# Earlier transfers in the first slots, and a later copy out of PSUM, in a fused attention and MLP kernel

## The chip, the core and the metric

The kernel runs on one core of a Trainium2 chip. The metric is the device time of one execution in microseconds (us); lower is better. PE (TensorE) multiplies matrices into PSUM; DVE (VectorE) and ACT (ScalarE) work element by element and are the ones here that read PSUM; POOL (GpSimd) works on SBUF alone. SP (SyncE), ACT and POOL can each issue DMA transfers, and the transfers that an engine issues stand in that engine's queue.

## The reference

Attention with a sliding window of 128 keys and a linear position bias, over 8 batches of 8 heads, 576 tokens and 64 channels, and on its output an MLP with a hard-swish:

```python
scores = scale * np.matmul(q, k.transpose(0, 1, 3, 2))
mask = (rel >= 0) & (rel < window)
scores = np.where(mask, scores + bias[None], -1000000000.0)
attn = np.exp(scores - max) / sum
x = np.matmul(attn, v)            # heads side by side: 4608 tokens x 512
h = x @ w_in                      # 512 x 2048
g = h * np.clip(h + 3.0, 0.0, 6.0) / 6.0
out = g @ w_out                   # 2048 x 512
```

All inputs and the output are float32 in DRAM; the kernel computes in bf16.

## The kernel before

**Slots.** Two heads are a pair; 32 pairs (8 batches of 4) are numbered g = 0 to 31. The kernel is a written-out order of instructions, one slot for each pair. Slots 0 to 4 are in `first_batch`, slots 5 to 31 in `segment`. In a slot, `scores(g)` computes the score tiles `scd` (diagonal blocks) and `sco` (the others), `exp_diag` and `exp_off` take their exponentials on ACT into `pd`, `po` and `p4buf` and mask them on POOL (L288, L298, L309), and `values(g - 1)` multiplies the pair before with v; DVE divides the result (L335, L336) into `avs`. `back` turns `avs` into columns of `xT`. Each engine does its instructions in the order in which they are written.

**q and k.** The pairs of batches 0 to 2 (g = 0 to 11) are loaded as contiguous runs with a cast to bf16 by `load_pairs` on POOL's DMA queue; `prepare(g)` reorders them in SBUF (`pr`, L217), `transposes(g)` turns them on PE (L234), and copies on DVE or ACT (L238) bring them from PSUM into `qTb` and `kTb`. For g of 9 to 11 both transposed tiles lie in one PSUM tile `tpp` of the pool `ps_sc`, which has two buffers and also serves `scd` and `sco`. From batch 3 on, q and k come as tokens over SP's queue (`load_tokens`, L121, five pieces of up to 256 KB), POOL casts them into the single buffer `tbuf` (L195), and a DMA transpose on SP (`xbar`, L200) writes `qTb` or `kTb`. So a cast into `tbuf` waits until the DMA transpose before it has read it. All v go over SP's queue too.

**Buffers.** `ldbuf[0]` to `ldbuf[3]` take all these loads in turn. `ldbuf[3]` holds pair 0 of batch 0 (`wide`) and then v of batch 1. In `stage_next(0)` a POOL memset of one element of `ldbuf[3]` stands ahead of the loads of v of batch 1, so that SP issues these only after POOL has come to it.

**MLP.** `moe_up` is four matmuls into `hps` (pool `ps_h`, two buffers), a ReLU on ACT into `r` (L373) and a DVE instruction into `g` (L374); `moe_down` is four matmuls (L401). These 288 units are taken in a fixed order by `fill`, in numbers fixed for each place of a slot: two in slot 4, then 4, 4, 3 and 3 in slots 5 to 8, eight in each later slot, and the rest at the end. A unit of 512 tokens needs the attention of those tokens done.

**Loads ahead.** `stage_next(g)` at the end of slot g issues loads: in slot 0 pairs 4 and 5 and v of batch 1, in slot 1 the first quarter of w_in, in slot 2 pairs 6 and 7, in slot 3 the second quarter of w_in, and so on until w_out has been loaded in slots 6 to 8. Weights and the pairs of the first three batches share POOL's queue, tokens and DMA transposes share SP's.

Of the kernel before, what the change touches and what calls it, by code (L numbers as in the profile page):

```python
# [18 lines left out]
def kernel(  # L19
# [9 lines left out]
    nc = tc.nc  # L29
    B, H, S, D = q.shape  # L30
# [5 lines left out]
    NP = H // 2  # L36
    NQ = 5
    LAST = S - 4 * 128
    SP = NQ * 128
    W = D + 1  # L40
# [70 lines left out]
    def flush(b=None, nm=None):  # L111
        while todo and (b is None or any(x[0] == (b, nm) for x in todo)):
            todo.pop(0)[1]()
# [12 lines left out]
    def constants():  # L126
        nc.vector.memset(bias3, 0.5)
        nc.vector.memset(warm, 0.0)
        nc.scalar.activation(out=warm, in_=warm, func=ACT.Exp)
        make_identity(nc, ident)  # L130
        for nm in "qk":
            load_pairs(0, nm, 1, 2)
        nc.gpsimd.iota(rel_i, pattern=[[0, 1]], base=0, channel_multiplier=1)
        base = rpool.tile([128, NT], FP32, tag="r6", name="base")
        base_i, base_b = base[:, 0:128].bitcast(INT32), base[:, 256:320].bitcast(BF16)
        nc.gpsimd.iota(base_i, pattern=[[0, 128]], base=-64, channel_multiplier=1)
        nc.gpsimd.tensor_copy(out=base_b, in_=base_i)
        nc.gpsimd.affine_select(out=base_b, in_=base_b, pattern=[[1, 128]],
                                channel_multiplier=-1, base=0,
                                compare_op=ALU.is_ge, fill=-(2.0 ** 30))  # L140
        for hp in range(2, NP):
            for nm in "qk":
                load_pairs(0, nm, hp, hp + 1)
        nc.vector.memset(kTb[0][:, :, 4, LAST:128], 0.0)
        nc.vector.memset(vbuf[0][:, :, :, D:W], 1.0)
        nc.vector.memset(vbuf[0][64:128, 4, :, 0:D], 0.0)
        nc.vector.memset(p4buf[0], 1.0)
        for h in range(H):
            nc.vector.tensor_scalar(out=tab[:, h, :], in0=base_b, scalar1=slopes[h] / scale,
                                    scalar2=0.0, op0=ALU.mult, op1=ALU.add)  # L150
        nc.gpsimd.memset(p4buf[1], 1.0)
        nc.gpsimd.memset(kTb[1][:, :, 4, LAST:128], 0.0)
        nc.gpsimd.memset(vbuf[1][:, :, :, D:W], 1.0)
        nc.gpsimd.memset(vbuf[1][64:128, 4, :, 0:D], 0.0)

    def biases():
        nc.vector.tensor_copy(out=rel_f, in_=rel_i)
        for h in range(H):
# [44 lines left out]
    st = {}  # L203
# [17 lines left out]
    def transposes(g):  # L221
        b, hp = divmod(g, NP)
        if g > 2 * NP:
            pair = ps_sc.tile([128, 2, 512], FP32, tag="sc", name="tpp")
        tps = {}
        for nm in "qk":
            src = st.pop((g, nm)).rearrange("p t e d -> p t (e d)")
            if g > 2 * NP:
                tp = pair[:, "qk".index(nm), 0:S // 2].bitcast(BF16).rearrange(
                    "p (t a) -> p t a", t=RT)  # L230
            else:
                tp = ps_h.tile([128, RT, RP], BF16, tag="h", name="tp", padded_shape=[128, 8, 128])
            for t in range(RT):
                nc.tensor.transpose(tp[:, t, :], src[:, t, :], ident[:RP, :RP])  # L234
            tps[nm] = tp
        for nm, dst in (("q", qTb[b % 2]), ("k", kTb[b % 2])):
            eng = nc.scalar.copy if nm == "k" and (g == 0 or g > 2 * NP) else nc.vector.tensor_copy
            eng(out=dst[:, hp, :, :].rearrange("p j c -> p (j c)")[:, 0:S].rearrange(  # L238
                "p (a t) -> p a t", t=RT), in_=tps[nm].rearrange("p t a -> p a t"))

# [194 lines left out]
    def stage_next(g):  # L435
        b, hp = divmod(g, NP)
        if g == 0:
            load_pairs(1, "q", 0, 2)
            load_pairs(1, "k", 0, 2)
            nc.gpsimd.memset(ldbuf[3][0:1, 0:1], 0.0)  # L440
            load_tokens(1, "v")
            flush()
        if g == 1:
            load_w_in(0)
        if g == 2:
            load_pairs(1, "q", 2, NP)
            load_pairs(1, "k", 2, NP)
        if g == 3:
            load_w_in(1)
        if g in (4, 5):  # L450
            load_w_in(g - 2)
            load_pairs(2, "q", 2 * (g - 4), 2 * (g - 3))
            load_pairs(2, "k", 2 * (g - 4), 2 * (g - 3))
        if g == 5:
            load_tokens(2, "v")
        if g == 6:
            load_w_out(0)
            load_w_out(1)
            load_tokens(3, "q")
        if g in (7, 8):  # L460
            load_w_out(g - 5)
        if g == 7:
            cast_tokens(2, "v")
            load_tokens(3, "k")
        if g == 8:
            cast_tokens(3, "q")
        if g == 9:
            load_tokens(3, "v")
            xbar(3, "q")
            cast_tokens(3, "k")  # L470
        if g == 10:
            xbar(3, "k")
            load_tokens(4, "q")
        if g == 11:
            cast_tokens(3, "v")
            load_tokens(4, "k")
            load_tokens(4, "v")
            cast_tokens(4, "q")
        if b >= 3 and b + 1 < B:
            if hp < 2:  # L480
                xbar(b + 1, "qk"[hp])
            if hp in (0, 2):
                cast_tokens(b + 1, "kkv"[hp])
        if b >= 3 and b + 2 < B:
            if hp > 0:
                load_tokens(b + 2, "qkv"[hp - 1])
            if hp == 3:
                cast_tokens(b + 2, "q")
# [6 lines left out]

    def first_batch():
        transposes(0)
        prepare(1)
        biases()
        for g in range(NP):  # L500
            if g != 2:
                scores(g)
            exp_diag(g, 0)
            spin(0)
            transposes(g + 1)
            exp_off(g, 0)
            exp_off(g, 1)
            if g == 1:
                for j in range(NQ):
                    cast_v(0, j, nc.scalar if j < 3 else nc.gpsimd)  # L510
                scores(2)
            prepare(g + 2)
            if g == 1:
                spin(0)
            if g > 0:
                values(g - 1, (0, 1, 2))
                values(g - 1, (3, 4))
            if g > 1:
                back(g - 2)
            if g == 2:  # L520
                more_constants()
            stage_next(g)
        g = NP
        scores(g)
        back(g - 2)
        values(g - 1, (0, 1, 2))
        values(g - 1, (3, 4))
        exp_diag(g, 0)
        for j in range(4):
            cast_v(1, j, nc.gpsimd)  # L530
        exp_off(g, 0)
        exp_off(g, 1)
        transposes(g + 1)
        back(g - 1)
        done[0] = g
        cast_v(1, 4, nc.gpsimd)
        prepare(g + 2)
        fill(1)
        stage_next(g)
        fill(1)  # L540

# [3 lines left out]
    def segment(lo, hi, fills):  # L545
        for g in range(lo, hi + 1):
            f = fills(g)
            if by_xbar(g - 2):
                done[0] = g - 1
            pe_next = g + 1 < hi and (g + 1) // NP < NB_PE  # L550
            if g < hi:
                scores(g)
            if pe_next and g < 2 * NP:
                transposes(g + 1)
            fill(f[0])
            if g < hi:
                exp_diag(g, 0)
            fill(f[1])
            if g < hi:
                exp_diag(g, 1)  # L560
            if g >= lo:
                values(g - 1, (0, 1, 2))
            fill(f[2])
            if pe_next and g >= 2 * NP:
                transposes(g + 1)
            if g < hi:
                exp_off(g, 0)
            fill(f[3])
            if g < hi:
                exp_off(g, 1)  # L570
            if g >= lo:
                values(g - 1, (3, 4))
            fill(f[4])
            if g >= lo:
                back(g - 1)
                if not by_xbar(g - 1):
                    done[0] = g
            if g + 2 < hi and (g + 2) // NP < NB_PE:
                prepare(g + 2)
            fill(f[5])  # L580
            if g < hi:
                stage_next(g)
            fill(f[6])
# [3 lines left out]
    with tc.manual_schedule(engines=every):  # L587
# [6 lines left out]
        for _ in range(30):  # L594
            nc.tensor.matmul(wm, lhsT=ident, rhs=ident, start=True, stop=True)
        prepare(0)
        first_batch()
        segment(NP + 1, G, lambda g: FILLS.get(g, (1, 1, 1, 1, 1, 1, 2)))
        done[0] = G
# [34 lines left out]
```

## Time and profile before

| | us |
|---|---|
| median of 4 runs | 341.62 (340.44 to 342.06) |
| the profiled execution | 341.8 |
| its span, first to last instruction | 340.1 |
| PE busy | 319.3 (94%) |
| ACT busy | 201.0 (59%) |
| DVE busy | 172.4 (51%) |
| POOL busy | 152.5 (45%) |
| granted TensorE clock | 1.000 |

The page cuts the span into 40 equal slices of 8.5 us and gives the busy share of each engine in tenths. The view of waits adds up how long an engine sat idle before an instruction and what released it. The chain of waits is followed back from the last instruction, at each step to what released it. The timeline lists instructions with their start and length, and in brackets the idle time ahead of them. The slots can be told by `scores`: slot 5 begins at 31.0 us, slot 8 at 51.0, 9 at 58.9, 10 at 70.1, 11 at 81.3, 12 at 90.4, 13 at 99.5 and 14 at 107.6. Queue q0 is POOL's, q1 is SP's, q10 is ACT's.

### The profile page before, as it was taken

To read this page: it belongs to the slowest core of one execution; us is meant where nothing else is said; L and a number is where in the kernel's file an instruction comes from. 1 tells how busy PE (TensorE), PEld (TensorE's weight loads), DVE (VectorE), ACT (ScalarE), POOL (GpSimd) and SP (SyncE) were. 2 spreads that over 40 slices of the span, in tenths; PEclk is the share of its full clock that TensorE was granted. 3 is DMA by queue.
4 is the path that set the end of the run, shared out by engine and by line. 5 is a ranking of instruction groups with operands and counts; after the bars stand their busy time and mean duration, and the time that the engine had idled before them with its cause. 6 is when DMAs were issued, how large, how long until landed. Compare 5 with 4: busy or idle time off the path is not lost.

```text
span 340.1 us, 6829 instructions
## 1 busy us (share of the span) xinstructions
PE 319.3 (94%) x2615; PEld 166.7 (49%) x2615; DVE 172.4 (51%) x358; ACT 201.0 (59%) x353; POOL 152.5 (45%) x263
## 2 busy tenths in 40 slices
PE   7887997897999999999999999999999999999995
PEld 5575554453444454554454444554555444444443
DVE  3677885554445455555455454545455444444410
ACT  3778776655657575767576757675765444343401
POOL 8779877635835663667366717632331000000000
PEclk9999999999999999999999999999999999999999
DMA  8999999999999999599959995410111000100021
GB/s 173 186 224 197 196 195 196 217 217 211 227 217 171 210 205 224 135 217 233 230 97 189 239 178 138 98 50 33 54 50 50 33 31 31 64 31 31 33 93 63
DMA packets 134832, 48.15 MB, mean 142 GB/s; under 512 B 121360, under 2 KB 130320, under 8 KB 134800
## 3 DMA queue, kind: packets, MB, share of 16 engines
q1 hardware_dynamic: 122464, 33.89, 55.2%
q0 software_dynamic: 8672, 7.44, 13.8%
q10 hardware_dynamic: 3664, 6.39, 5.5%
q8 instruction: 20, 0.33, 0.4%
q14 instruction: 12, 0.10, 0.1%
HBM read 36.70 MB, written 9.44 MB: 136 GB/s over the span
## 4 chain that ended last, share of the span: by engine, by line
PE 64%; SPq 8%; ACT 7%; DVE 6%; POOL 5%; issue 5%; DMA 3%; POOLq 0%
PE hps L369 28%; PE ops L401 26%; SPq L121 6%; DVE g L374 3%; ACT r L373 3%; ACT po L295 2%; DMA ldbuf<-in_k_dram 2%; POOL pd L288 2%; SPq L200 2%; POOL tbuf L195 2%; PE av L330 2%; PE scd L265 1%; PE av L327 1%; DVE qTb L238 1%; DVE avs L336 1%
## 5 line engine op out<-in xcount | busy, mean ns | idle before, releaser
L374 DVE SCALAR_TENSOR_TENSOR g<-r,hps 128x512 bf16<-128x512 f32 x144 | 99.0, 688 | 137.0 <-ACT r L373 136.9
L373 ACT ACTIVATE r<-hps,bias 128x512 f32<-128x512 f32 x144 | 99.5, 692 | 104.9 <-PE hps L369 102.8
L369 PE MATMUL hps<-xT,w_in_sb 128*128 128x512 bf16 x576 | 146.9, 379 | 9.5 <-DVE g L374 9.3
L401 PE MATMUL ops<-w_out_sb,g 128*128 128x512 bf16 x560 | 141.8, 379 | 0.0
L401 PEld LDWEIGHTS <-g 128*128 128x128 bf16 x560 | 54.3, 98 | 63.5
L369 PEld LDWEIGHTS <-w_in_sb 128*128 128x128 bf16 x576 | 50.8, 97 | 62.5 <-issue 12.6
L298 POOL TENSOR_SCALAR_AFFINE_SELECT po<-po 128x512 bf16<-128x512 bf16 x64 | 40.0, 635 | 22.5 <-ACT po L295 20.0
L288 POOL TENSOR_SCALAR_AFFINE_SELECT pd<-pd 128x512 bf16<-128x512 bf16 x46 | 28.1, 635 | 39.8 <-ACT pd L285 39.8
L195 POOL CAST tbuf<-ldbuf 128x512 bf16<-128x512 f32 (+1 forms) x50 | 28.6, 614 | 36.8 <-issue 25.0
L295 ACT ACTIVATE po<-sco,bias_o 128x512 bf16<-128x512 f32 x64 | 43.1, 689 | 0.0
L336 DVE TENSOR_TENSOR avs<-av,rc 128x384 bf16<-128x384 f32 (+1 forms) x56 | 28.0, 501 | 1.9
L285 ACT ACTIVATE pd<-scd,bias_d 128x512 bf16<-128x512 f32 x46 | 29.0, 685 | 0.0
L330 PEld LDWEIGHTS <-pd 128*128 128x128 bf16 x256 | 19.3, 99 | 9.4 <-issue 0.7
L327 PE MATMUL av<-vbuf,po 128*128 128x65 bf16 x224 | 21.6, 195 | 0.7 <-POOL po L298 0.6
L330 PE MATMUL av<-vbuf,pd 128*128 128x65 bf16 x240 | 22.0, 196 | 0.0
L327 PEld LDWEIGHTS <-po 128*128 128x128 bf16 x256 | 19.5, 100 | 3.9 <-POOL po L298 1.1
L407 ACT COPY osb<-ops 128x512 f32<-128x512 f32 x18 | 10.6, 586 | 12.7 <-PE ops L401 12.6
L217 POOL COPY pr<-ldbuf 96x768 bf16<-96x768 bf16 x17 | 13.7, 822 | 4.6 <-DMA ldbuf<-in_k_dram 3.9
L306 ACT ACTIVATE p4buf<-sco,bias_d 128x64 bf16<-128x64 f32 x46 | 14.9, 324 | 0.0
L409 DVE COPY osb<-ops 128x512 f32<-128x512 f32 x17 | 11.6, 684 | 5.8 <-PE ops L401 5.8
L265 PE MATMUL scd<-qTb,kTb 64*128 64x128 bf16 x256 | 13.3, 227 | 0.0
L234 PE MATMUL tp<-ident,pr 96*128 96x96 bf16 x108 | 9.2, 243 | 3.8 <-POOL pr L217 1.0
(76 smaller groups left out, 222.0 us busy)
## 6 DMA issues: line engine op xcount, KB each, us to landing
ldbuf<-in_v_dram SPq DMA_DIRECT2D x32, 256.0 KB, 5.4
out_dram<-osb ACTq DMA_DIRECT2D x23, 256.0 KB, 3.6
ldbuf<-in_q_dram SPq DMA_DIRECT2D x20, 256.0 KB, 5.2
ldbuf<-in_k_dram SPq DMA_DIRECT2D x20, 256.0 KB, 5.8
out_dram<-osb SPq DMA_DIRECT2D x12, 256.0 KB, 2.0
w_in_sb<-in_moe_w_in_dram POOLq DMA_DIRECT2D x4, 512.0 KB, 8.5
w_out_sb<-in_moe_w_out_dram POOLq DMA_DIRECT2D x4, 512.0 KB, 11.1
ldbuf<-in_q_dram POOLq DMA_DIRECT2D x4, 288.0 KB, 8.8
```

The costliest lines, as they stand in the source:

```text
L195: nc.gpsimd.tensor_copy(out=tbuf[:m, :, j, :], in_=s[:m, j, :, :].rearrange("p (i e) d -> p i (e d)", e=2))
L285: nc.scalar.activation(out=pd[:, e, :, :].rearrange("p j c -> p (j c)"), in_=sc[:, e, :], func=ACT.Exp, bias=bias_d[:, h:h + 1], scale=scale)
L288: nc.gpsimd.affine_select(out=pd[:, e, :, :], in_=pd[:, e, :, :], pattern=[[0, 4], [1, 128]], channel_multiplier=-1, base=0, compare_op=AL ...
L295: nc.scalar.activation(out=po[:, e, :, :].rearrange("p j c -> p (j c)"), in_=sc[:, e, :], func=ACT.Exp, bias=bias_o[:, h:h + 1], scale=scale)
L298: nc.gpsimd.affine_select(out=po[:, e, :, :], in_=po[:, e, :, :], pattern=[[0, 4], [-1, 128]], channel_multiplier=1, base=-1, compare_op=A ...
L327: nc.tensor.matmul(av[:, i, e, :], lhsT=po[:, e, qt - 1, :], rhs=vb[:, qt - 1, h, :], start=True, stop=False)
L330: nc.tensor.matmul(av[:, i, e, :], lhsT=d, rhs=vb[:, qt, h, :], start=(qt == 0), stop=True)
L336: nc.vector.tensor_tensor(out=st[g, "avs"][:, qts[0]:qts[0] + nq, :, :], in0=av[:, 0:nq, :, 0:D], in1=rc[:, 0:nq, :, :].to_broadcast([128, ...
L369: nc.tensor.matmul(hps, lhsT=w_in_sb[:, ks, ts(ms, 128)], rhs=xT[:, ks, ts(nt, NT)], start=(ks == 0), stop=(ks == n_ks - 1))
L373: nc.scalar.activation(out=r6, in_=hps, func=ACT.Relu, bias=bias3[:, 0:1], scale=1.0 / 6.0)
L374: nc.vector.scalar_tensor_tensor(out=gts[nt][:, ms, :], in0=r6, scalar=1.0, in1=hps, op0=ALU.min, op1=ALU.mult)
L401: nc.tensor.matmul(ops[nt, sub], lhsT=gts[nt][:, ms, ts(sub, 128)], rhs=w_out_sb[:, ms, :], start=(ms == 0), stop=(ms == n_ms - 1))
```

## The change

There are four edits. The loads of v of batch 1 move from the end of slot 0 to the place right after `prepare(0)`, and the one-element memset goes. The first quarter of w_in is issued in slot 0 instead of slot 1, and pairs 6 and 7 in slot 1 instead of slot 2. Four memsets of the second set of buffers move from POOL to DVE, ahead of the eight instructions that write `tab`. The copies from PSUM become a function `settle`: for pairs 9, 10 and 11 it runs after the second half of `values` instead of right behind the transposes, and the copy of k, until now on ACT for these pairs, is on DVE like that of q. For all other pairs `settle` follows `transposes` directly, on the same engines as before.

```diff
         nc.vector.memset(p4buf[0], 1.0)
+        nc.vector.memset(p4buf[1], 1.0)
+        nc.vector.memset(kTb[1][:, :, 4, LAST:128], 0.0)
+        nc.vector.memset(vbuf[1][:, :, :, D:W], 1.0)
+        nc.vector.memset(vbuf[1][64:128, 4, :, 0:D], 0.0)
         for h in range(H):
             nc.vector.tensor_scalar(out=tab[:, h, :], in0=base_b, scalar1=slopes[h] / scale,
                                     scalar2=0.0, op0=ALU.mult, op1=ALU.add)
-        nc.gpsimd.memset(p4buf[1], 1.0)
-        nc.gpsimd.memset(kTb[1][:, :, 4, LAST:128], 0.0)
-        nc.gpsimd.memset(vbuf[1][:, :, :, D:W], 1.0)
-        nc.gpsimd.memset(vbuf[1][64:128, 4, :, 0:D], 0.0)
...
             tps[nm] = tp
+        st[g, "tps"] = tps
+
+    def settle(g):
+        b, hp = divmod(g, NP)
+        tps = st.pop((g, "tps"))
         for nm, dst in (("q", qTb[b % 2]), ("k", kTb[b % 2])):
-            eng = nc.scalar.copy if nm == "k" and (g == 0 or g > 2 * NP) else nc.vector.tensor_copy
+            eng = nc.scalar.copy if nm == "k" and g == 0 else nc.vector.tensor_copy
...
         if g == 0:
             load_pairs(1, "q", 0, 2)
             load_pairs(1, "k", 0, 2)
-            nc.gpsimd.memset(ldbuf[3][0:1, 0:1], 0.0)
-            load_tokens(1, "v")
-            flush()
+            load_w_in(0)
         if g == 1:
-            load_w_in(0)
-        if g == 2:
             load_pairs(1, "q", 2, NP)
             load_pairs(1, "k", 2, NP)
...
                 values(g - 1, (3, 4))
+            if pe_next and g >= 2 * NP:
+                settle(g + 1)
             fill(f[4])
...
         prepare(0)
+        load_tokens(1, "v")
+        flush()
         first_batch()
```

## The prediction

> **What bounds the kernel now.** I read the page's slices first.
>
> ```profile
> PE   7887997897999999999999999999999999999995
> DMA  8999999999999999599959995410111000100021
> ```
>
> From the twelfth slice (93 us) on PE is full, so what it does there (2.6 thousand matmuls, none of them touched) keeps its length; the change can only move the start of that stretch. But the DMA engines are full too for the first 24 slices. Next the waits in slots 8 to 11 (50 to 82 us), PE's first, ACT's second:
>
> ```profile
> PE hps L369 <- DVE g L374: 5.8, 4, 1.9
> ```
> ```profile
> ACT kTb L238 <- DVE qTb L238: 4.4, 3, 1.6
> ```
>
> PE stands 5.8 us, in three waits of 1.9 us and a small one. The timeline of slot 9 shows why:
>
> ```profile
> 63.92 0.75 DVE L238 COPY qTb<-tpp 128x576 bf16<-128x576 bf16 x1
> ...
> 64.70 0.64 ACT L238 COPY kTb<-tpp 128x576 bf16<-128x576 bf16 x1 [1.42 <-DVE qTb L238]
> ...
> 65.24 0.69 ACT L295 ACTIVATE po<-sco,bias_o 128x512 bf16<-128x512 f32 x1
> ...
> 66.78 0.72 ACT L373 ACTIVATE r<-hps,bias 128x512 f32<-128x512 f32 x1
> ...
> 67.53 0.69 DVE L374 SCALAR_TENSOR_TENSOR g<-r,hps 128x512 bf16<-128x512 f32 x1 [2.31 <-ACT r L373]
> ...
> 68.27 1.02 PE L369 MATMUL hps<-xT,w_in_sb 128*128 128x512 bf16 x4 [1.85 <-DVE g L374]
> ```
>
> ACT stands 1.42 us at its copy of k until DVE has copied q; both exponentials, r, g and at last PE come late by that and by the copy. Then the chain of waits of 68 to 112 us, to see what a sooner PE meets:
>
> ```profile
> 96.90 1.11 SPq L121
> ...
> 98.20 4.15 SPq L200
> 102.39 3.64 DMA ldbuf<-in_v_dram
> ...
> 108.36 1.18 POOL pd L288 x2
> 109.54 1.19 POOL po L298 x2
> 110.77 0.20 PE av L327
> ```
> ```profile
> 105.52 2.84 POOL L195 CAST tbuf<-ldbuf 128x512 bf16<-128x512 f32 x5 [8.46 <-DMA qTb<-tbuf]
> ```
>
> SP issues loads without a pause up to the DMA transpose of q of batch 4 at 98.20; POOL idles 8.46 us for that one to land, casts k, and only then masks pd and po of slot 13. PE, in slot 14, waits 0.35 us for them at 110.77. So at 110 us two paths arrive almost together: PE's, and SP's queue through `tbuf`. That second one decides my forecast.
>
> **The copies (settle).** Behind the change ACT goes from r straight to the exponentials; both copies follow the second values on DVE. Slot 9 worked out: r ends 63.28; two exponentials and two of p4 (65.24 to 66.9, 1.67) end 64.95; r of the next unit follows its matmuls (65.1) and ends 65.9. DVE: g to 64.0, the division of values (0.17 + 0.42, matmuls done 64.3) to 65.0, q 0.75, k 0.70 (it was 0.64 on ACT, 0.66 as a second copy on DVE in slot 6), then g 0.69 at 66.45 to 67.15. PE goes on at 67.2 instead of 68.27: **1.1 us**. Slot 10 has the same rows 11.16 us on: 1.1. Slot 8 the same way (copies 54.85 to 56.3, g to 57.0 instead of 57.93): 0.9. DVE has the 2 x 0.7 us free (it idles 2.31 ahead of g); if it hadn't, g would be late by them. `tpp` is held 1.5 us longer; the next to want its buffer is sco of the next slot (70.09 less the gain, against 66.4), so nobody waits. Sum 3.1 us.
>
> **The loads.** POOL's queue keeps its order: pairs 4 and 5, w_in's first quarter, pairs 6 and 7, w_in's second. Only the issue moves. w_in's 0.76 us of issue comes at 14.19, ahead of POOL's masks, in the place of a memset of 0.09; they began at 14.79, so 0.16 late, and the casts of v behind them (to 17.25) too; PE needs the last at 17.50. I take 0; bare it is 0.16. In slot 1 the pairs' 1.35 us take the place of w_in's 0.76 and end at 19.5; the next mask began at 19.41. Pairs 6 and 7 land some 4 us sooner; POOL's `pr` of k at 32.53 waited 0.56 for them, and PE's transposes of pair 6 behind it 0.83: **0.6 us** in slot 5. PE's lead at slot 14 is 3.1 + 0.6 = 3.7 us.
>
> v of batch 1 was issued at 14.29, after 3.6 us of idle SP (its queue was free at 10.65, `prepare(0)` was done at 6.29). What that is worth for SP's path, the busy times by window say (last column: GB/s):
>
> ```profile
> 13.50:15.50 2.00, 1.87 (x14) 1.11 (x14) 1.42 (x3) 2.00 (x5) 1.48 (x5) 1.00 0.76 98
> 16.00:18.00 2.00, 2.00 (x39) 1.86 (x34) 0.74 (x3) 1.28 (x3) 2.00 (x5) 1.00 1.31 201
> 18.50:20.00 1.50, 1.07 (x18) 1.10 (x19) 1.34 (x3) 1.50 (x5) 0.81 (x3) 1.00 1.32 259
> 42.00:58.00 16.00, 13.09 (x152) 7.65 (x151) 11.58 (x25) 11.31 (x18) 11.62 (x17) 1.00 1.24 195
> ```
>
> At 16 to 18 us POOL's queue has the engines alone (201), at 18.5 to 20 SP's (259). From 13.5 to 15.5 they run at 98: against 201 or 259 that is 1.0 to 1.2 us lost, and v would fill it. From 20.5 to 22 (183 GB/s), where w_in's queue starts anew after a break, a further 0.3 to 0.8 is lost; with w_in queued already the break is gone. Against it: 16 to 20.5 us would be shared. In 42 to 58 both move 2.39 and 0.70 MB, 149/201 + 44/259 = 0.91 of what they move one after the other: 0.09 x 4.5 = 0.4 us lost. **SP's path sooner by 1.1 + 0.5 - 0.4 = 1.2 us.** Unseen, so bounded: at most 3.6 (the issue itself); at least -1.5 (below). Nearest is the gap's own row, so 1.2.
>
> Will v land late? Two rows:
>
> ```profile
> q0 software_dynamic: 538, 0.40, 130.1%
> q1 hardware_dynamic: 13, 0.00, 0.9%
> ```
>
> From 16 to 18 us SP's queue, with some 0.5 MB issued, moved 13 packets; from 42 to 58 2799 against POOL's 2682. By the second, v ends near 27.5 us, in time for POOL's casts (27.18 to 31.2). By the first it waits until POOL's queue is empty near 26.5, and ends at 29: casts and pair 6 late by some 1.5, PE's lead 2.2 instead of 3.7, still over 1.2.
> The Trainium skill (DMA: Bandwidth & Descriptors, Queues, rings and completion order) says that a DMA engine takes turns between its queues packet by packet. The counts of 42 to 58 us agree, those of 16 to 18 don't; by the rule v is in time, by the row PE's lead shrinks, and the forecast is the same.
>
> **The memsets.** On DVE 0.27 + 0.17 + 0.09 + 0.48 = 1.0 us by the rows of the first set; they fill the 1.74 us that DVE idles ahead of `tab` (4.08). POOL saves 1.38 us (6.51 to 7.89) ahead of an idle 2.09: nothing. If they held up POOL (its first DMA issue, under DVE's 0.48 memset, took 0.77, the next 0.64) `tab` would come up to 1.0 late: taken from PE's lead, not from the end. I take 0.
> The Trainium skill (SBUF — State Buffer, SBUF: two separate sides) warns that DVE in a two-port mode keeps POOL from writing DMA descriptors, which speaks against this edit; by it up to the memsets' 1.0 us is lost. No row here shows more than those 0.13 us.
>
> **Sum.** PE comes to slot 14 3.7 us sooner, POOL's po 1.2: PE then waits 0.35 + 2.5 = 2.9 us there. SP's next round (the second transpose at 108.39, the loads of batch 5) hangs on the same cast, so all later slots move by 1.2 and no more. From the profiled execution 341.8 - 1.2 = 340.6 (span 338.9); it lies 0.2 above the median, so **340.4**.
>
> **Rivals.**
> 1. *The whole lead passes*: SP's queue gains as much as PE, since it may begin 3.6 us sooner. Against it, SP is held by full engines all the way to 98 us. 341.6 - 3.5 = 338.1. Chance 0.15.
> 2. *Nothing reaches the end*: PE, sooner, stores its output sooner, and one more store (0.26 MB at 259 GB/s, 1.0 us) stands ahead of the transpose at 98 us. 1.2 - 1.0 = 0.2: 341.4. Chance 0.27.
> 3. *Slower, by SP's path*: POOL's queue, served early, runs empty twice (near 27 us until w_in's second quarter, near 32 until its third, whose issue stays in slots 3 and 4), and each restart costs like 13.5 to 15.5, 1.1 us. 2 x 1.1 + 0.4 - 1.1 = 1.5 later: 343.1. For it: 34.5 to 36.5 has only 178 GB/s. Against: a break near 25.8 and one at 35 are in the trace of before too. It decides once new restarts and the sharing cost more than the 1.1 recovered in the gap. Chance 0.10.
>
> **How the numbers follow.** The forecast has 0.48. A measurement of this kernel can't tell less than 0.3% (1.0 us) from no change; 1.2 is near that edge, so I give 0.40 of it to faster, 0.08 to the same. Faster 0.40 + 0.15 = 0.55; same 0.08 + 0.27 = 0.35; slower 0.10. The range takes in rival 2 and most of rival 1 and leaves out rival 3: 338.2 to 342.3.
>
> **What would show it.** Right: waits of PE on g in slots 8 to 10 of 0.8 instead of 1.9 us, ACT's wait at kTb gone; no slice at 98 GB/s near 14 us; the transpose of q of batch 4 near 97; PE waiting some 3 us on po in slot 14. Wrong: no such wait (rival 1), the transpose at 98 or later (2, 3), k's copy delaying g by more than ACT's did.

## The result and the profile after

The changed kernel took 343.22 us (median of 43 runs, 341.40 to 344.78); the kernel before took 342.38 us in the 62 runs beside it (339.47 to 345.52). The ratio is 1.0029, 95% interval 1.0015 to 1.0043: 1.0 us slower, about the least that can be told from no change. The forecast was 1.2 us faster. The profiled execution has a span of 341.9 us (before: 340.1) and a mean granted clock of 0.985 (1.000).

The slices of the page after:

```profile
PE   6865998989989899999999999999999999999995
PEclk9699899999999999999999999999999999999999
DMA  9999999999999999599959996410111000100021
```

DMA is as full as before up to the 24th slice. PE falls short in the fourth (25.6 to 34.2 us). The clock row before is 9 throughout (not rightly so at the start, see the ledger); it is now 6 in the second slice and 8 in the fifth, behind PE's shortfall. PE's waits:

```profile
PE tp L233 <- POOL pr L216: 6.0, 4, 3.1
PE hps L373 <- DVE g L378: 5.6, 13, 0.7
```

The waits of 1.9 us on `g` are gone (longest 0.7; the sum was 9.3, now 5.6). In their place PE waits for reordered pairs (`pr`), 3.1 us in one piece. That piece is in slot 5; POOL's timeline shows what stands ahead of `pr`, after and then before:

```profile
26.24 1.17 POOL L180 CAST vbuf<-ldbuf 128x512 bf16<-128x512 f32 x2
29.92 0.62 POOL L180 CAST vbuf<-ldbuf 128x512 bf16<-128x512 f32 x1 [2.50 <-DMA ldbuf<-in_v_dram]
...
33.39 1.59 POOL L216 COPY pr<-ldbuf 96x768 bf16<-96x768 bf16 x2
34.93 0.76 POOL L168 DMA_DIRECT2D w_in_sb<-in_moe_w_in_dram  x1
```
```profile
27.18 2.28 POOL L181 CAST vbuf<-ldbuf 128x512 bf16<-128x512 f32 x4
```

v of batch 1, issued sooner, lands later: its last piece at 32.8 us instead of 28.1. The casts wait 3.2 us for it in four pieces (before: not at all), and `pr` of pair 6 and the issue of w_in's third quarter stand behind them in POOL's order. That issue was at 33.30 and is at 34.93. POOL's queue had run dry at 33.8 by its packets and moved nothing until 36.8. Busy times by window, after (last columns: granted clock, DMA share, GB/s):

```profile
32.00:34.00 2.00, 0.00 (x0) 0.00 (x0) 0.00 (x0) 1.41 (x4) 1.80 (x4) 1.00 0.58 123
36.50:39.50 3.00, 3.00 (x13) 1.19 (x12) 1.65 (x4) 0.74 (x2) 3.00 (x5) 0.56 1.16 193
```

The first row had 209 GB/s before. The second shows what else PE's pause cost: from 36.5 to 39.5 us the granted clock is 0.56. PE's timeline after and then before, the same eight matmuls of slot 5:

```profile
34.27 0.43 PE L233 MATMUL tp<-ident,pr 96*128 96x96 bf16 x6 [3.11 <-POOL pr L216]
...
35.97 3.44 PE L373 MATMUL hps<-xT,w_in_sb 128*128 128x512 bf16 x8
```
```profile
34.22 1.89 PE L369 MATMUL hps<-xT,w_in_sb 128*128 128x512 bf16 x8
```

**The ledger.** The start of each slot's `scores`, after less before, gives the whole account in microseconds:

| stretch | change | what it is |
|---|---|---|
| up to slot 5 | -1.06 | starts 29.95 instead of 31.01 (see below) |
| slot 5 | +4.36 | waits on `pr` 3.45 instead of one of 0.83 (2.6), and 3.44 - 1.89 = 1.55 by the lower clock |
| slots 8, 9, 10 | -1.26, -1.37, -0.43 | the later copies |
| slot 12 | +0.95 | a late store on ACT (below) |
| slot 14 | +1.07 | masks behind the cast into `tbuf`: waits of 1.11 instead of 0.35 |
| slot 26 | -0.45 | |
| slot 31 | +1.78 | where it stands in all; as the spans: 341.9 - 340.1 = 1.8 |

The first row can't be put down to the change. PE's timelines of slot 3, before and then after, have the same two matmuls:

```profile
20.88 1.06 PE L253 MATMUL scd<-tab,ident 128*128 128x512 bf16 x2
```
```profile
19.27 0.59 PE L257 MATMUL scd<-tab,ident 128*128 128x512 bf16 x2
```

They take 0.59 us at full clock. In the profile of before they take 1.06 us up to 20.88 and 0.59 from 24.98 on, so PE ran at about half speed there until past 21 us, though the clock row says 9 and the mean 1.000; after, they take 1.05 us for the last time at 13.68. The kernel before has a second profile (span 339.4 us). It starts slot 5 at 29.89, as soon as the changed kernel does, and slot 6 at 37.28 against 41.77.

The rows of slots 5 to 12 add up to 2.25 us. Less the 1.06 of the first row, PE comes to slot 14 1.2 us later, where the forecast had it 3.7 us sooner.

SP's path, after: the DMA transpose of q of batch 4 is later, not sooner (98.20 before), and so is the cast behind it (105.52 before).

```profile
100.05 4.32 SPq L199 DMA_TRANSPOSE qTb<-tbuf  x1
```
```profile
107.78 2.83 POOL L194 CAST tbuf<-ldbuf 128x512 bf16<-128x512 f32 x5 [9.55 <-DMA qTb<-tbuf]
```

How SP's queue fell behind can be read from the megabytes landed by a given time, from the packets of both traces:

| landed by | 15.5 us | 26 us | 32 us | 37 us | 98 us |
|---|---|---|---|---|---|
| POOL's queue, before / after | 0.95 / 0.92 | 2.00 / 2.49 | 2.75 / 3.09 | 3.21 / 3.12 | 7.44 / 7.44 |
| SP's queue, before / after | 1.47 / 1.70 | 2.71 / 2.15 | 3.10 / 2.92 | 3.63 / 3.65 | 11.35 / 11.03 |
| after less before, both | +0.20 | -0.07 | +0.16 | -0.07 | -0.32 |

At 15.5 us the sooner v has filled the gap (+0.23 MB). By 26 us SP's queue is 0.56 MB behind: that is v. From 26 to 32 us v catches up. From 32 to 37 us the dry queue takes that back. At 98 us POOL's queue stands equal and SP's lacks 0.32 MB, some 1.6 us at 0.2 MB per us.

### The profile page after: what moved, and what is told of

Same layout as the page of the kernel before. It is cut to its first block, busy times and chain, and to the rows that moved or that the text cites. A ratio compares the mean times of both kernels' runs of the same rounds, so it can differ in the third digit from the quotient of the medians.

```text
span 341.9 us, 6826 instructions
## 1 busy us (share of the span) xinstructions
PE 317.4 (93%) x2615; PEld 163.7 (48%) x2615; DVE 176.1 (52%) x365; ACT 199.2 (58%) x350; POOL 150.8 (44%) x258
## 3 DMA queue, kind: packets, MB, share of 16 engines
q0 software_dynamic: 8672, 7.44, 13.6%
## 4 chain that ended last, share of the span: by engine, by line
PE 63%; DMA 18%; ACT 6%; POOL 5%; DVE 3%; issue 2%; SPq 2%; ACTq 0%; POOLq 0%
PE ops L405 28%; PE hps L373 27%; DMA ldbuf<-in_q_dram 7%; DMA ldbuf<-in_k_dram 7%; DMA ldbuf<-in_v_dram 4%; ACT r L377 2%; SPq L121 2%; DVE g L378 2%; ACT pd L289 2%; POOL pd L292 2%; ACT po L299 2%; PE av L334 1%; PE scd L269 1%; PE av L331 1%; PE ops L389 1%
## 5 line engine op out<-in xcount | busy, mean ns | idle before, releaser
L373 PE MATMUL hps<-xT,w_in_sb 128*128 128x512 bf16 x576 | 148.6, 382 | 5.8 <-DVE g L378 5.6
L334 PEld LDWEIGHTS <-pd 128*128 128x128 bf16 x256 | 18.6, 97 | 9.6 <-POOL pd L292 1.0
L331 PEld LDWEIGHTS <-po 128*128 128x128 bf16 x256 | 18.8, 98 | 5.4 <-DVE avs L340 1.0
L411 ACT COPY osb<-ops 128x512 f32<-128x512 f32 x18 | 10.5, 585 | 12.8 <-PE ops L405 12.8
L233 PE MATMUL tp<-ident,pr 96*128 96x96 bf16 x108 | 8.2, 222 | 8.9 <-POOL pr L216 6.0
L233 PEld LDWEIGHTS <-pr 96*128 96x128 bf16 x144 | 7.7, 104 | 13.0 <-POOL pr L216 7.4
```

The source lines that it names most:

```text
L331: nc.tensor.matmul(av[:, i, e, :], lhsT=po[:, e, qt - 1, :], rhs=vb[:, qt - 1, h, :], start=True, stop=False)
L334: nc.tensor.matmul(av[:, i, e, :], lhsT=d, rhs=vb[:, qt, h, :], start=(qt == 0), stop=True)
L373: nc.tensor.matmul(hps, lhsT=w_in_sb[:, ks, ts(ms, 128)], rhs=xT[:, ks, ts(nt, NT)], start=(ks == 0), stop=(ks == n_ks - 1))
```

## The experiments

Two theories. **A**: the end is set by SP's path, and what the change does to that is decided by the queueing of w_in and the pairs on POOL's queue; PE's gain from the copies is real but doesn't reach the end. **B**: the copies themselves, or the memsets, cost something.

**e1, the copies alone** (before, with `settle` and nothing else of the change):

```diff
+            if pe_next and g >= 2 * NP:
+                settle(g + 1)
             fill(f[4])
```

> Kernel before with the later copies (settle, pairs 9 to 11, both on DVE) and nothing else. Theory (SP's path through tbuf sets the end): slots 8 to 11 shorten by 3.1 us together, as they do between the two profiles, the DMA transpose of q of batch 4 stays at 98.2 us, PE's wait on the masks in slot 14 grows from 0.35 to about 3.4, and the time is that of before within 0.7 us. Rival (PE's own path sets the end and SP's follows it): 3 us less than before.

Measured: 343.10 us, ratio 1.0022 (0.9989 to 1.0054). Slots 8 and 9 gain 1.25 and 1.27 us; at the end nothing is left. That speaks against B, which would need a loss in those slots. The time is as A forecast it, but the trace does not test A: v of batch 1 was late here too (casts wait 2.8 us), with the unchanged early order, so that isn't the change's alone. PE came to slot 14 not 3 us sooner but 0.8 us later, the transpose of q of batch 4 was at 99.79 and not at 98.2, and PE waited 0.7 us there for masks and not 3.4.

**e2, the queueing undone** (the changed kernel, w_in's first quarter and pairs 6 and 7 back in their slots):

```diff
-            load_w_in(0)
         if g == 1:
+            load_w_in(0)
+        if g == 2:
             load_pairs(1, "q", 2, NP)
```

> Changed kernel, but w_in's first quarter and pairs 6 and 7 issued in slots 1 and 2 again; v of batch 1 stays early. Theory (v of batch 1 is starved by the transfers that the change queues on POOL's queue): v then shares the engines with pairs 4 and 5 alone and lands before 25 us, POOL's casts in slot 4 don't wait (3.0 us in the changed kernel), w_in's third quarter is issued near 33 instead of 34.9, the transpose of q of batch 4 is near 97.5, the time 0.5 to 1.5 us under before. Rival (issuing v early is itself what costs): the casts still wait and the time is that of the changed kernel, 1 to 2 us over before.

Measured: 342.14 us, ratio 0.9992 (0.9962 to 1.0023); v on time (casts wait 0.2 us), slot 6 at +0.02. The time is short of the 0.5 to 1.5 us under before that were forecast: PE was 2.6 us ahead at slot 10 and lost 1.8 of it there to a late store on ACT (below). The copies and the memsets are in this kernel, which speaks against B too. The same kernel was run again beside the changed one:

> Changed kernel with the queueing undone (w_in's first quarter in slot 1, pairs 6 and 7 in slot 2; early v, memsets and later copies kept), a second time. Theory: casts wait under 0.5 us again, slot 6 begins within 1 us of 39.06, and the time is 0.5 to 2 us under the changed kernel's in the same rounds. Rival: casts wait 1.5 us or more here too, and the time is the changed kernel's.

> The changed kernel again, for a second profile and beside the next two on the same chip. Theory (with w_in and pairs 6 and 7 queued early, v of batch 1 is late in every execution): POOL's casts in slot 4 wait over 1.5 us for it, slot 6 begins 3 us or more behind 39.06, and the time is 0 to 1.5 us over before. Rival (late or not is a matter of the execution): casts wait under 0.5 us and slot 6 begins at 38 to 39.

Measured: 340.99 us (0.9954, 0.9929 to 0.9979) against 342.93 us (1.0027, 0.9990 to 1.0063) for the changed kernel, whose casts waited 4.7 us, with slot 6 at +3.84. So the queueing costs 1.9 us in these rounds, and here the intervals do not overlap. The casts of e2 waited 0.5 us. Its slot 6 was not on time all the same, at +1.89, outside the 1 us forecast: two waits of 1.0 us on `pr` in slot 5 and a granted clock of 0.50 behind them. The two results for e2 differ by more than one would like; both are below the changed kernel's.

**e3, the queue kept from running dry** (the changed kernel, w_in's third quarter issued right behind the second, ahead of the casts):

```diff
         if g == 3:
             load_w_in(1)
+            load_w_in(2)
```

> Changed kernel with w_in's third quarter issued in slot 3, right behind the second, so that its issue no longer stands behind POOL's casts of v. Theory (two effects: the late casts delay PE in slot 5, and through the late issue POOL's queue stands empty from 33.7 to 36.8 us): the casts and PE's 4 us in slot 5 stay, the empty stretch goes, the transpose of q of batch 4 comes 1 to 1.9 us sooner than 100.05, and the time is within 1 us of before, about 1.3 under the changed kernel. Rival (PE's late slot 5 sets the end): time of the changed kernel.

```profile
25.62 1.51 POOL L168 DMA_DIRECT2D w_in_sb<-in_moe_w_in_dram  x2
...
29.59 0.62 POOL L180 CAST vbuf<-ldbuf 128x512 bf16<-128x512 f32 x1 [1.29 <-DMA ldbuf<-in_v_dram]
```
```profile
96.23 4.23 SPq L199 DMA_TRANSPOSE qTb<-tbuf  x1
```

POOL's and SP's timelines: both issues stand ahead of the casts, the empty stretch is gone, and the transpose comes at 96.23 instead of 100.05, twice as much sooner as forecast. Slot 6 is still 3.5 us late (casts wait 1.7), so PE's loss in slot 5 and the empty stretch are two things, both behind POOL's waiting casts. The time, 341.86 us (1.0002, 0.9970 to 1.0033), is 0.9 us below the changed kernel's by the ratios; the intervals overlap, and one trace is no proof where two of before differ by 2.8 us at this transpose.

**e4, the queueing alone** (before, with w_in's first quarter in slot 0 behind v, and pairs 6 and 7 in slot 1):

```diff
             flush()
-        if g == 1:
             load_w_in(0)
-        if g == 2:
+        if g == 1:
```

> Kernel before with only w_in's first quarter queued in slot 0 and pairs 6 and 7 in slot 1; v of batch 1 still waits for POOL's memset. Theory: v is starved as in the changed kernel or worse and lands at 30 us or later, POOL's casts wait 3 us or more, slot 6 begins 3 to 4 us late and, without the later copies, nothing wins that back: time 3 to 5 us over before. Rival (the early v is what takes the bandwidth from the pairs): time within 1 us of before.

Measured: 344.68 us, ratio 1.0074 (1.0036 to 1.0112). This is the clearest loss, 2.5 us by the ratio, if less than the 3 to 5 forecast. Casts wait 3.4 us, slot 6 is at +3.29, and with no copies to win it back that stays (+3.26 at slot 13). The transpose is at 96.56, sooner than before: in this kernel PE's path sets the end. That goes against the first half of A. POOL's queue stood empty here too, for 5.4 us up to 36.9, and SP's path was not late.

**e5 to e7, SP's path relieved.** If SP's path is what hides the copies' gain, a shorter one must let it through. v of batches 4 to 7, which stood ahead of the transpose of q on SP's queue, goes behind it:

```diff
-            load_tokens(4, "v")
             cast_tokens(4, "q")
         if b >= 3 and b + 1 < B:
             if hp < 2:
                 xbar(b + 1, "qk"[hp])
+            if hp == 0:
+                load_tokens(b + 1, "v")
...
-            if hp > 0:
-                load_tokens(b + 2, "qkv"[hp - 1])
+            if hp in (1, 2):
+                load_tokens(b + 2, "qk"[hp - 1])
```

e5 is before with this; e6 is e1 with it; e7 is e3 with it.

> Kernel before, with the loads of v of batches 4 to 7 issued behind the DMA transpose of q of the same batch instead of ahead of it; nothing else. Theory (in slot 14 SP's path through tbuf and PE's path come within 0.4 us of each other): SP's path is 3 to 4 us shorter there (transpose near 94.5), PE gains only its waits on the masks in slots 14 and 26, 0.4 + 0.4, so 0 to 1 us under before. Rival (SP's path alone sets the end): 3 us or more under before.

> The later copies alone, and v of batches 4 to 7 behind the transpose as in the run of that alone. Theory: with SP's path shortened the 3.1 us of the copies reach the end: 2.5 to 4 us under before, much more than the copies alone (none) and the moved loads alone (0 to 1) together. Rival (the copies bring nothing to PE, or another path ends just behind SP's): within 1 us of before.

> Changed kernel with w_in's third quarter in slot 3 and v of batches 4 to 7 behind the transpose. Theory: SP's path no longer binds, so the time is that of PE's path: the copies' 3.1 us gained, the 3.5 us lost in slots 4 and 5 to the late v of batch 1 not, about 0 to 1 us under before and 2 to 4 over the run with the copies and the moved loads alone. Rival (SP's path decides still, and the changed loads help it): 3 us or more under before.

| ratio to before | v ahead | v behind |
|---|---|---|
| copies as before | 1 | 1.0018 (0.9988 to 1.0049) |
| copies later | 1.0022 (0.9989 to 1.0054) | 0.9949 (0.9923 to 0.9976) |

Each alone brings nothing; together they bring 0.5%. (The ratios are each to the kernel before in the same rounds.) Two paths arrive almost together, as the prediction read from the profile, and only moving both moves the end. The times are 342.64 us for e5 and 340.29 us for e6; e6 gains 1.7 us where 2.5 to 4 were forecast, and e5 is 0.6 us over before instead of up to 1 under, which is within its interval. e7 has the lowest time of all, 339.13 us (7 runs), ratio 0.9922 (0.9889 to 0.9956); its transpose is at 91.31. That is below both kernels, though its interval overlaps those of e6 and e8. Its forecast, up to 1 us under before and 2 to 4 over e6, missed: slot 6 was 2.0 us late instead of 3.5, and its stores did not wait (below).

**e8, all that had helped** (e2, with w_in's third quarter ahead as in e3, and v behind as in e5):

> The changed kernel with the queueing undone, w_in's third quarter in slot 3, and v of batches 4 to 7 behind the DMA transpose of q. Theory: v on time (slot 6 near 39) and SP's path out of the way, so PE keeps the copies' 3.1 us: 3 to 4.5 us under before, and 0.5 to 2 under the run with the queueing kept (2.7 under before). Rival (PE's late slot 5 wasn't what kept that run back): within 0.4 us of it.

Measured: 340.31 us (0.9935, 0.9903 to 0.9967), 2.2 us under before instead of 3 to 4.5, and no better than e7. v was on time (slot 6 at -0.97) and PE had a lead of 3.6 us at slot 10; then slot 10 lost 4.1. ACT's timeline in e8:

```profile
66.60 0.59 ACT L411 COPY osb<-ops 128x512 f32<-128x512 f32 x1 [0.17 <-PE ops L405]
71.01 0.37 ACTq L415 DMA_DIRECT2D out_dram<-osb  x1
71.48 0.69 ACT L377 ACTIVATE r<-hps,bias 128x512 f32<-128x512 f32 x1 [4.30 <-DMA ldbuf<-in_k_dram]
```

The output tile is in `osb` at 67.19, yet ACT issues its store only at 71.01, and r, put down to a load of k, and PE's transposes (3.1 us) wait behind it. r itself needs nothing of k: it reads `hps` and a bias that every r before it had read. So it must be the store that waited. A load of k on SP's queue landed at 70.93, 0.08 us ahead of the store. The changed kernel pays for this as well, in slots 10 and 12; its ACT timeline in slot 12:

```profile
90.73 0.59 ACT L411 COPY osb<-ops 128x512 f32<-128x512 f32 x1 [0.17 <-PE ops L405]
93.07 0.34 ACTq L415 DMA_DIRECT2D out_dram<-osb  x1
93.51 0.69 ACT L377 ACTIVATE r<-hps,bias 128x512 f32<-128x512 f32 x1 [2.19 <-PE av L334]
```

93.07 - 91.32 = 1.75 us; in the kernel before the store of that place followed its copy within 0.2 us. In seven traces (both of the changed kernel and of e2, and those of e1, e6 and e8) twelve stores of slots 10 and 12 were 0.5 to 3.8 us late, and each was issued 0.08 us after a load of k or q on SP's queue had landed. All seven have the later copies; e3 and e7 have them too and no late store. Two last runs put the stores behind the slot's exponentials, e10 in e8 and e11 in the changed kernel:

```diff
-            while stores:
+            while stores and not hold:
                 stores.pop(0)()
...
+            hold.append(1)
             fill(f[0])
...
+            hold.clear()
             fill(f[4])
```

> e8_best with each output store issued behind the slot's exponentials instead of ahead of them. Store theory: in slot 10 of e8_best ACT stood 4.3 us because the store, not the ReLU behind it, waited for a load on SP's queue; issued some 5 us later the store finds the load landed, PE keeps its lead through slots 10 to 12 (slot 11 some 4 us sooner than in e8_best, 81.75 to about 77.7), the DMA transpose of q of batch 4 stays near 94 and still hides, and the end comes 3 to 4 us sooner: 336.3 to 337.3 us. Rival, the ReLU or the exponentials themselves wait for that load or for PE: slot 11 within 0.5 us of e8_best and 340.3 us.

> The changed kernel with the same later stores and nothing else. Store theory: slots 10 and 12 each lose 0.95 us less in a profile where v is as late as in the changed kernel's, so PE comes to slot 14 1.9 us sooner; but the masks there still stand behind SP's DMA transpose near 100 us, so PE waits that much more for them and the end moves by 0.5 us at most: 342.5 to 343.3 us. Rival, PE's lead does reach the end: 341.3 us. Rival, the ACT waits are not the store's: slot starts 10 to 13 and the time as before the edit, 343.0 us.

Measured: 340.81 us (0.9955, 0.9925 to 0.9985) for e10 and 343.45 us (1.0022, 0.9990 to 1.0054) for e11. e10 misses its forecast by 3.5 us, e11 is just outside. ACT's timeline of e10:

```profile
76.59 0.37 ACTq L416 DMA_DIRECT2D out_dram<-osb  x1
77.06 0.69 ACT L378 ACTIVATE r<-hps,bias 128x512 f32<-128x512 f32 x1 [3.49 <-DMA ldbuf<-in_v_dram]
```

The wait went with the store: ACT stands 3.5 us again (3.6 in e11), at the store's new place, until 0.08 us after a load of v has landed, which SP issues behind those of k. So the wait is the store's and not that of the ReLU or the exponentials, and a later place does not escape it. Why the store is tied to a load of another queue, the runs don't show; a place without the tie was not found, so its worth was not measured at the end.

## Why the prediction was wrong, step by step

- **The copies: right in mechanism, a little low in size.** Forecast 0.9 + 1.1 + 1.1 = 3.1 us; the ledger gives 1.26 + 1.37 + 0.43 = 3.06. That the sums agree is chance: in e7, whose stores did not wait, the three are 1.26, 1.37 and 1.38 (4.0), and in the changed kernel the store took 0.95 of the last one. The copies of slot 9 did not delay `g`, as worked out; the timeline after:

```profile
66.88 0.75 DVE L242 COPY qTb<-tpp 128x576 bf16<-128x576 bf16 x1
...
67.55 0.75 DVE L242 COPY kTb<-tpp 128x576 bf16<-128x576 bf16 x1
68.21 0.68 DVE L378 SCALAR_TENSOR_TENSOR g<-r,hps 128x512 bf16<-128x512 f32 x1
...
68.94 0.38 PE L373 MATMUL hps<-xT,w_in_sb 128*128 128x512 bf16 x1 [0.65 <-DVE g L378]
```

- **"That second one decides my forecast": right as far as a lead goes.** The two-by-two of e6 shows that what the copies win does not pass while SP's path is as late as this. e4 shows the other side: there PE is the later of the two. And in the changed kernel there was no lead: 1.2 of the 1.8 us at the end PE brought to slot 14 itself, and the masks there and in slot 26 add 0.6 (1.07 - 0.45).
- **"SP's path sooner by 1.1 + 0.5 - 0.4 = 1.2 us": the step that failed.** The profile has it 1.85 us later (the transpose at 100.05 instead of 98.20; 99.47 in the second profile of the changed kernel). The 1.1 is there: at 189 instead of 98 GB/s, 0.20 MB more by 15.5 us. What follows was mis-sized. I let the queues share from 16 to 20.5 us and set 0.4 against the 0.5 of the restart. They shared up to 26 us and beyond, because w_in's quarter and pairs 6 and 7, some 1.1 MB, now stood in one row: 194 instead of 217 GB/s over 10.5 us, 10.5 x (1 - 194/217) = 1.1 us lost where I had 0.1 gained. The loss per microsecond was about as I had it, 151/201 + 43/259 = 0.92; it was the length that I had wrong. The queues of the DMA view after, 15.5 to 26 us (packets, MB, share):

```profile
q0 software_dynamic: 1953, 1.58, 95.8%
q1 hardware_dynamic: 1770, 0.45, 30.1%
```

  And a term was missing: the dry queue of 32 to 37 us, 155 instead of 201 GB/s, 5 x (1 - 155/201) = 1.1 us. In this profile it took back what v's catching up had won. It is no fixed price: in the changed kernel's second profile POOL's queue stood empty for 5.0 us and in e4 for 5.4, and the engines still moved 199 and 202 GB/s from 32 to 37 us, since SP's queue filled them. The last 0.25 MB of the 0.32 are lost in small pieces between 37 and 98 us, and I can't put them down to one place; two profiles of before differ by more (98.20 and 95.41). So the 1.2 us did not come, the longer sharing is measured, and most of the 1.85 us stays open.
- **"v in time or 1.5 us late, and the forecast is the same": wrong twice.** The last piece of v landed at 32.8 us, 4.6 later than before and 3.8 later than the 29 of my worse case (the last cast at 32.84 instead of 30.59). And I priced the lateness on PE's lead alone. POOL also issues DMAs: what stands behind its waiting casts is w_in's third quarter, and its queue was left dry. e3 takes that wait away, and its transpose is 3.8 us sooner; that the dry queue is what makes SP's path late is not shown, since e4 had it dry for longer with the transpose at 96.56. The wait was to be asked of everything queued behind it on POOL, and I asked it only of `pr`.
- **The Trainium skill** (DMA: Bandwidth & Descriptors, Queues, rings and completion order) says that an engine alternates between its queues packet by packet. The two rows above agree, by packets as the profile counts them: 1953 against 1770. The first 2 us of the sharing don't, from 16 to 18 us it was 469 against 90. What I drew from it was too kind: with turns by packet the queue with the larger packets (809 bytes against 254 on average) takes 3.5 times the bytes, and v crawls at 0.45 MB in 10.5 us, 43 GB/s.
- **Slot 5's 0.6: wrong sign,** +4.36, and with it "PE's lead at slot 14 is 3.1 + 0.6 = 3.7 us": it was 1.2 late. This is the better shown of the two failures: e4 adds the queueing and loses 2.5 us; e2 takes it away, the casts no longer wait for v, and slot 6 is 1.4 to 3.8 us sooner than in the changed kernel's two profiles. 1.55 of it is a price I did not have at all: the clock (below).
- **The memsets: right.** They fill DVE's idle time, `tab` still starts at 4.08, and POOL's DMA issue under them takes 0.77 and 0.63 us as before.
- **Rival 3** had an empty POOL queue ahead of w_in's third quarter, which came, and a time (343.1) within 0.2 of the median. That the time fits so well is luck: rival 3 did not have PE's loss in slot 5. I gave it 0.10 since an empty stretch near 25.8 and a break near 35 us were in the trace of before too. I should have asked what would lengthen them.
- **A number misread:** the 2.6 thousand matmuls of the first paragraph are those of the whole program, not of the full stretch; nothing rests on it.
- **One trace of before was too good.** It had v on time, and so had its second profile (waits of 0.5 us, slot 6 at 37.28). But e1, e5 and e6, with the same order in slots 0 to 7, waited 2.8 to 3.5 us for v. With the queueing v was late in 6 of 6 profiles; with it undone and v issued early, in 0 of 4; in the original order, in 3 of 5 (late: over 1 us of waits). So the change seems to trade an occasional loss for a steady one, which would be why the ledger's 1.8 us are 1.0 by the ratio of all runs. What makes v late in some executions of the original order stays open.

## What to carry to other kernels

Before transfers are issued sooner, count the bytes of both queues until the first consumer of the other queue needs its data; here the queue with the larger packets took 1.58 MB while the other got 0.45. When a wait is added on an engine that also issues DMAs, price the DMAs behind it, not only its computed tiles: issuing them ahead of the wait (e3, e7) cost nothing that the times show and kept the queue from standing empty there. And when two paths arrive together, test them as a two-by-two, since each improvement alone can look worthless, as here.

## What the runs showed of the hardware

- **A pause of PE costs more than its length.** In the changed kernel a pause of 3.11 us, over at 34.27, was followed by a granted clock of 0.56 from 36.5 to 39.5 us, and eight matmuls took 1.55 us longer. In e4, e5 and the changed kernel's second profile, pauses of 3.4 to 4.9 us were followed by 0.50 from 37 to 39 us; before, with no wait over 0.83 us there, the clock stayed at 1.00 and the same matmuls took 1.89 us. The Trainium skill (TensorE: Matmul & The Clock Gate, Part 1: The HAM clock gate) has the clock halve after an idle window of about 3.4 us. The size agrees. The threshold reads too long: in e7 a pause of 2.15 us was followed by 0.52, and in the second profile of e2, where two waits of 1.0 us were the longest and PE was busy for 3.0 of the 5 us from 30 to 35, by 0.50.
- **A store can wait for another queue's load.** An output store on ACT was issued up to 3.8 us after its data were ready (e8), 0.08 us after the landing of a load that SP had issued; moved, it went out behind the landing of a different one, with ACT idle for 3.5 us.
- **The clock row can lack a stretch.** The profile of before shows a clock of 1.00 up to 21 us, where the same matmuls took 1.06 us instead of 0.59.
- **The same program loads unevenly.** Two profiles of the kernel before have the same DMA transpose at 98.20 and 95.41 us, with 0.2% between their spans.
